# Attention scores of one head at a time, in two halves of the array's rows, in place of head pairs on a block-diagonal key matrix

## The chip, the cores and the metric

The kernel runs on one core of one Trainium2 chip. The metric is the device time of one execution in microseconds (us); lower is better. Three runs of the kernel before took 1596.24 to 1597.06 us, median 1596.8 us.

## What is computed

The reference runs attention with pooled keys and values, then two feed-forward blocks. Cut to what matters here:

```python
B, H, S, D = 8, 8, 576, 64             # pool = 8, so Sp = 72 keys for each head
k_p = k.reshape(B, H, Sp, pool, D).mean(axis=3)
v_p = v.reshape(B, H, Sp, pool, D).mean(axis=3)
scores = scale * np.matmul(q, k_p.transpose(0, 1, 3, 2))
attn = softmax(scores)
x = np.matmul(attn, v_p)               # to 4608 tokens x 512
h = ((x @ w1) * (x @ w2)) @ w3
x2 = h @ w_out
g = softplus(x2 @ w_in)
out = g @ moe2_w_out
```

## The kernel before

**Stages.** The 4608 tokens are 36 attention groups of 128 tokens and 9 blocks of 512 tokens. First (`W_mm`, line 374) the product of w3 and w_out is formed, in plain fp32, while weights arrive by DMA and are converted by ScalarE and VectorE. Then comes the first feed-forward block (`ab`, `x2_mm`, through `mm3`, lines 82 to 84), in which each product is three fp32r matmuls of 128x128 by 512 columns. Attention is spread over both stages: a table of slots (`sched`, filled by `at`) says in which slot each step of each group is recorded, and `p1_step` calls three slots for every 36 matmuls of the feed-forward block. The last stage (`h_mm`, `o_mm`) has no attention in it. Each engine works in the order in which its instructions were recorded.

**One attention group** has, in this order and some slots apart: `scores` (line 205), `softmax` (218), `normalize`, `p_transpose` (line 244, tile `pTp`), `pv` (line 262) and `x_split` (lines 78 and 79, tiles `xh` and `xl`). Four groups are in the first stage, 32 in the feed-forward stage. A group of 128 tokens can straddle two batches, since a batch has 576 tokens: `segments` then returns two pieces of 64 tokens. This is so for 4 of the 36 groups, called crossing groups below; the other 32 are plain.

**Scores.** Queries arrive transposed as `q` [128 rows, 4, 256 tokens]: the rows of slice m are the 64 dimensions of head 2m and the 64 of head 2m+1. `pool_k` sums the raw keys by eight with one VectorE reduction for each m into `ks`, and two ScalarE copies (line 193) put its upper and lower 64 rows on the diagonal of `kT`, whose other blocks were zeroed once by GpSimd (line 337). One matmul of 128 rows, 128 query columns as weights and 144 moving columns then gives two heads (line 213). Four matmuls make a plain group: m = 0 and 1 into the first PSUM tile of the group, m = 2 and 3 into the second. An fp32 matmul is two instructions on the engine, so a plain group has 8 of them, each with its own weight load, and a crossing group 16 (of 64 weight columns).

**PSUM.** `at_p` holds two banks, which scores, transposes and `pv` take in turn. The second score tile of a group is the bank that `pv` of the group before it used, free when `x_split` has read it.

`pv` is a model for the split of the array: head h has its 64 result rows at 64*(h % 2), so even and odd heads multiply in the left and right 64 columns of the array:

```python
r = 64 * (h % 2)
nc.tensor.matmul(ps[r:r + 64, c:c + n], vb_t[b][:, h, :], pT[:, h, o:o + n], start=True, stop=True)
```

Of the kernel before, what the change touches and what calls it, by code (L numbers as in the profile page):

```python
# [8 lines left out]
F32 = mybir.dt.float32  # L9
F32R = mybir.dt.float32r  # L10
I32 = mybir.dt.int32
AF = mybir.ActivationFunctionType
ALU = mybir.AluOpType
AX = mybir.AxisListType

P = 128
B, H, S, D = 8, 8, 576, 64
POOL = 8
SP = S // POOL
# [10 lines left out]
SCALE = 1.0 / (D**0.5 * POOL)  # L30
# [10 lines left out]
def segments(g):  # L41

    b, r = divmod(g * P, S)
    n = min(P, S - r)
    return [(b, 0, n)] + ([(b + 1, n, P - n)] if n < P else [])
# [3 lines left out]
def pooled_attention_two_ffn(ctx: ExitStack, tc: tile.TileContext, qT_d, kT_d, v_d, w12_d, w3T_d, wo_d, wi_d, wo2_d, out):  # L49
# [3 lines left out]
    nc = tc.nc  # L53
# [16 lines left out]
    def at_tile(name):  # L70
        return at_p.tile([P, 512], F32, tag="at", name=name)
# [93 lines left out]
    ap_ = att_stack.enter_context(tc.tile_pool(name="att", bufs=1))  # L165
    q_t, kT_t, vb_t, kv_raw = {}, {}, {}, {}
# [13 lines left out]
            nc.sync.dma_start(t, v_d[b, :, 2 * POOL * D * c:2 * POOL * D * (c + 1)])  # L180
        kv_raw[b, which, c] = t

    kT_bufs = [ap_.tile([P, 4, 2 * SP], F32, tag=f"kT{i}", name=f"kT{i}") for i in range(2)]

    def pool_k(b, m):

        raw = kv_raw.pop((b, 0, m))
        kT_t[b] = kT_bufs[b % 2]
        sums = ap_.tile([P, SP], F32, tag="ksum", name=f"ks{b}_{m}", bufs=2)
        nc.vector.tensor_reduce(sums, raw.rearrange("p (s o) -> p s o", o=POOL), axis=AX.X, op=ALU.add)  # L190
        for i in range(2):
            r = slice(64 * i, 64 * i + 64)
            nc.scalar.activation(kT_t[b][r, m, SP * i:SP * i + SP], sums[r], AF.Copy)

    def pool_v(b, c):

# [6 lines left out]
    sc_t, pr_t, pT_t, pv_t = {}, {}, {}, {}  # L203

    def scores(g):
        q = q_t[g // 2]
        q0 = P * (g % 2)
        sc_t[g] = [at_tile(f"sc{g}_{half}") for half in range(2)]
        for half in range(2):
            ps = sc_t[g][half]  # L210
            for b, o, n in segments(g):
                for m in (2 * half, 2 * half + 1):
                    nc.tensor.matmul(  # L213
                        ps[o:o + n, 2 * SP * (m % 2):2 * SP * (m % 2) + 2 * SP], q[:, m, q0 + o:q0 + o + n], kT_t[b][:, m, :],
                        start=True, stop=True,
                    )

    def softmax(g):
        pr = ap_.tile([P, H, SP], F32, tag="pr", name=f"pr{g}", bufs=2)
        mx = ap_.tile([P, H], F32, tag="mx", name=f"mx{g}", bufs=2)  # L220
        sm = ap_.tile([P, H], F32, tag="sm", name=f"sm{g}", bufs=2)
        sc = [ps[:, :4 * SP].rearrange("p (h n) -> p h n", n=SP) for ps in sc_t.pop(g)]
        for half in range(2):
            nc.vector.tensor_reduce(mx[:, 4 * half:4 * half + 4], sc[half], axis=AX.X, op=ALU.max)
        nc.vector.tensor_scalar(mx, mx, -SCALE, None, op0=ALU.mult)  # L225
        for h in range(H):
            nc.scalar.activation(pr[:, h, :], sc[h // 4][:, h % 4, :], AF.Exp, bias=mx[:, h:h + 1], scale=SCALE, accum_out=sm[:, h:h + 1])  # L227
        pr_t[g] = pr, sm

    def normalize(g):  # L230
# [48 lines left out]
    def kv_step():  # L279
        b, w, c = kv_pieces[kv_pooled[0]]  # L280
        (pool_v if w else pool_k)(b, c)
        kv_pooled[0] += 1
        kv_load_to(kv_pooled[0] + 3)
# [16 lines left out]
    for g in range(NG):  # L300
        o = STEPS_FIRST if g < 4 else STEPS_DENSE if g < 8 or g >= NG - 4 else STEPS
        if o[3] < o[4]:
            at(begin[g] + o[4], lambda g=g: x_split(g))
        at(begin[g], lambda g=g: scores(g))
        at(begin[g] + o[0], lambda g=g: softmax(g))
        at(begin[g] + o[1], lambda g=g: normalize(g))
        at(begin[g] + o[2], lambda g=g: p_transpose(g))
        at(begin[g] + o[3], lambda g=g: pv(g))
        if o[3] == o[4]:
            at(begin[g] + o[3], lambda g=g: x_split(g))  # L310
        if g % 2 == 1 and g // 2 + 3 < NG // 2:
            at(begin[g] + 1, lambda g=g: load_q(g // 2 + 3))
# [20 lines left out]
    with tc.manual_schedule():  # L333
        nc.scalar.preload_act_table_set("natural_log_exp_and_others")
        make_identity(nc, ident)
        for t in kT_bufs:
            nc.gpsimd.memset(t, 0.0)

# [246 lines left out]
        for n in range(len(seq) + LAG):  # L587
            if n < len(seq):
                j, f = seq[n]
# [64 lines left out]
```

## Time and profile before

| | before |
|---|---|
| median of 3 runs | 1596.8 us |
| profiled execution | 1598.61 us |
| its span, first to last instruction | 1596.8 us |
| PE busy (matmul) | 1556.2 us, 97% of the span |
| PEld busy (weight load) | 1254.9 us, 79% |
| VectorE (DVE) / ScalarE (ACT) busy | 853.7 us / 799.7 us |
| mean granted TensorE clock | 0.996 |

Times in the profile are from the first instruction of the span. Matmuls are pipelined: the duration of one matmul instruction reaches past the start of the next, so costs on PE are read from the distance between starts. `L213` is line 213 of the kernel; `sc<-kT,q` is a matmul that writes tile `sc` from tiles `kT` and `q`; `128*64` after a matmul is rows by columns of the array in use, `128x144` what moves through it, and `x8` how many instructions a row merges.

### The profile page before, as it was taken

What the parts mean: (1) busy time and instruction counts of PE and PEld (TensorE: products, weight loads), DVE (VectorE), ACT (ScalarE), POOL (GpSimd) and SP (SyncE); (2) the same over time, 40 slices, a digit from 0 to 9 for tenths busy, and PEclk for the clock granted to TensorE, in tenths of its full rate; (3) what the DMA queues carried; (4) which work ended last, traced back from release to release, by engine and by line L of the source; (5) the groups of instructions that cost most, each with busy time, mean ns of one, the idle gap of its engine ahead of it and who ended that gap; (6) DMA issues with size and microseconds to landing.
All of it is one profiled execution on the core that took longest, in us unless ns stands there. A gap on an engine that the chain in (4) does not pass through costs nothing.

```text
span 1596.8 us, 19269 instructions
## 1 busy us (share of the span) xinstructions
PE 1556.2 (97%) x7424; PEld 1254.9 (79%) x7424; DVE 853.7 (53%) x1452; ACT 799.7 (50%) x1813; POOL 1.7 (0%) x8
## 2 busy tenths in 40 slices
PE   4898999999999999999999999999999999999999
PEld 2457888888888888878878888888888888888887
DVE  6896534243433434327878755555555555555554
ACT  3555433343434343334467665556565565565554
POOL 0000000000000000000000000000000000000000
PEclk9999999999999999999999999999999999999999
DMA  8652212021212111204341101000000001010000
GB/s 275 212 185 76 90 46 66 25 76 37 77 36 63 52 62 29 79 1 158 132 132 54 53 1 53 1 27 27 27 27 27 27 1 53 1 53 1 7 20 27
DMA packets 32011, 95.61 MB, mean 60 GB/s; under 512 B 3632, under 2 KB 3632, under 8 KB 30768
## 3 DMA queue, kind: packets, MB, share of 16 engines
q1 hardware_dynamic: 31920, 94.39, 18.1%
q8 instruction: 58, 0.95, 0.3%
q14 instruction: 33, 0.27, 0.1%
HBM read 75.50 MB, written 18.87 MB: 59 GB/s over the span
## 4 chain that ended last, share of the span: by engine, by line
PE 84%; DVE 8%; ACT 4%; DMA 2%; issue 1%; SPq 0%; ACTq 0%; DVEq 0%
PE ab L82 8%; PE o L573 7%; PE ab L84 7%; PE ab L83 7%; PE o L575 7%; PE o L574 7%; PE h L82 7%; PE h L83 7%; PE h L84 7%; PE x2p L82 4%; PE x2p L84 4%; PE x2p L83 4%; PE sc L213 2%; PE pv L262 2%; PE pTp L244 2%; DMA raw_w<-in_w3T_dram 1%
## 5 line engine op out<-in xcount | busy, mean ns | idle before, releaser
L79 DVE TENSOR_TENSOR g2l<-d,g2h 128x512 fp32r<-128x512 f32 x144 | 99.6, 692 | 328.9 <-ACT g2h L78 328.9
L573 PE MATMUL o<-w2h,g2h 128*128 128x512 f32 x576 | 224.8, 390 | 1.8 <-DVE x2s L445 1.7
L575 PE MATMUL o<-w2h,g2l 128*128 128x512 f32 x576 | 224.2, 389 | 0.0
L574 PE MATMUL o<-w2l,g2h 128*128 128x512 f32 x576 | 224.2, 389 | 0.0
L543 ACT ACTIVATE e<-h 128x512 f32<-128x512 f32 x144 | 85.8, 596 | 270.2 <-PE h L84 270.2
L78 ACT ACTIVATE gh<-g 128x512 fp32r<-128x512 f32 x72 | 45.5, 633 | 179.1 <-DVE g L428 179.1
L573 PEld LDWEIGHTS o<-w2h,g2h 128*128 128x128 f32 x576 | 108.1, 188 | 26.6 <-DVE x2s L445 2.1
L575 PEld LDWEIGHTS o<-w2h,g2l 128*128 128x128 f32 x576 | 108.1, 188 | 23.0 <-DVE g2l L79 0.4
L574 PEld LDWEIGHTS o<-w2l,g2h 128*128 128x128 f32 x576 | 108.1, 188 | 21.8
L82 PE MATMUL x2p<-gh,Wh 128*128 128x512 f32 x288 | 116.1, 403 | 0.0
L84 PE MATMUL x2p<-gh,Wl 128*128 128x512 f32 x288 | 112.6, 391 | 0.0
L83 PE MATMUL x2p<-gl,Wh 128*128 128x512 f32 x288 | 112.3, 390 | 0.0
L227 ACT ACTIVATE pr<-sc,mx 128x72 f32<-128x72 f32 x288 | 87.7, 331 | 48.8 <-DVE mx L225 48.7
L428 DVE TENSOR_TENSOR g<-a,ab 128x512 f32<-128x512 f32 x72 | 49.4, 686 | 108.1 <-PE ab L84 107.0
L553 DVE TENSOR_TENSOR d<-d,l 128x512 f32<-128x512 f32 x144 | 99.7, 692 | 5.0
L552 DVE SCALAR_TENSOR_TENSOR d<-h,d 128x512 f32<-128x512 f32 x144 | 99.6, 692 | 5.0
L551 DVE SCALAR_TENSOR_TENSOR d<-u,e 128x512 f32<-128x512 f32 x144 | 98.7, 685 | 1.0 <-ACT u L546 1.0
L79 DVE TENSOR_TENSOR xl<-pv,xh 128x512 fp32r<-128x512 f32 x36 | 24.8, 690 | 135.5 <-ACT xh L78 135.5
L546 ACT ACTIVATE u<-e 128x512 f32<-128x512 f32 x144 | 91.0, 632 | 10.1 <-DVE d L551 5.7
L548 ACT ACTIVATE l<-u 128x512 f32<-128x512 f32 x144 | 91.1, 633 | 4.7
L544 ACT ACTIVATE e<-e 128x512 f32<-128x512 f32 x144 | 91.0, 632 | 4.6
L78 ACT ACTIVATE g2h<-d 128x512 fp32r<-128x512 f32 x144 | 88.6, 615 | 3.5 <-DVE d L553 2.8
(207 smaller groups left out, 3209.7 us busy)
## 6 DMA issues: line engine op xcount, KB each, us to landing
raw_wo<-in_wo_dram SPq DMA_DIRECT2D x24, 512.0 KB
kv<-in_kT_dram SPq DMA_DIRECT2D x32, 288.0 KB
q<-in_qT_dram SPq DMA_DIRECT2D x18, 512.0 KB
kv<-in_v_dram SPq DMA_DIRECT2D x32, 288.0 KB
x2d<-x2s SPq DMA_DIRECT2D x36, 256.0 KB
x2r<-x2d SPq DMA_DIRECT2D x9, 1024.0 KB
out_dram<-os SPq DMA_DIRECT2D x36, 256.0 KB
raw_w<-in_w3T_dram SPq DMA_DIRECT2D x16, 512.0 KB
```

The lines of the kernel that those rows point to most:

```text
L78: nc.scalar.activation(hi, src, AF.Copy)
L79: nc.vector.tensor_sub(lo, src, hi.bitcast(F32))
L82: nc.tensor.matmul(ps, whi, xhi, start=first, stop=False)
L83: nc.tensor.matmul(ps, whi, xlo, start=False, stop=False)
L84: nc.tensor.matmul(ps, wlo, xhi, start=False, stop=last)
L548: nc.scalar.activation(ln, u, AF.Ln)
L551: nc.vector.scalar_tensor_tensor(d, u, 1.0, e, op0=ALU.subtract, op1=ALU.subtract)
L552: nc.vector.scalar_tensor_tensor(d, ps, 0.0, d, op0=ALU.max, op1=ALU.subtract)
L553: nc.vector.tensor_add(d, d, ln)
L573: nc.tensor.matmul(oacc[j][t], hi[:, s_], wh, start=f == 0, stop=False)
L574: nc.tensor.matmul(oacc[j][t], hi[:, s_], wl, start=False, stop=False)
L575: nc.tensor.matmul(oacc[j][t], lo[:, s_], wh, start=False, stop=f == K2 - 1)
```

## The change

`pool_k` reduces straight into a `kT` tile [128, 4, 72] without zero blocks; the two ScalarE copies, the tile `ks` and the GpSimd zeroing go. `scores` runs over segments, then m, then i: the 64 rows of head 2m+i of the queries against the 64 rows of its keys, 72 moving columns, into PSUM tile i. Even heads are in the first tile of a group and odd heads in the second, and `softmax` reads them from there.

```diff
-    kT_bufs = [ap_.tile([P, 4, 2 * SP], F32, tag=f"kT{i}", name=f"kT{i}") for i in range(2)]
...
-        kT_t[b] = kT_bufs[b % 2]
-        sums = ap_.tile([P, SP], F32, tag="ksum", name=f"ks{b}_{m}", bufs=2)
-        nc.vector.tensor_reduce(sums, raw.rearrange("p (s o) -> p s o", o=POOL), axis=AX.X, op=ALU.add)
-        for i in range(2):
-            r = slice(64 * i, 64 * i + 64)
-            nc.scalar.activation(kT_t[b][r, m, SP * i:SP * i + SP], sums[r], AF.Copy)
+        if m == 0:
+            kT_t[b] = ap_.tile([P, 4, SP], F32, tag="kT", name=f"kT{b}", bufs=2)
+        nc.vector.tensor_reduce(kT_t[b][:, m, :], raw.rearrange("p (s o) -> p s o", o=POOL), axis=AX.X, op=ALU.add)
...
-        sc_t[g] = [at_tile(f"sc{g}_{half}") for half in range(2)]
-        for half in range(2):
-            ps = sc_t[g][half]
-            for b, o, n in segments(g):
-                for m in (2 * half, 2 * half + 1):
+        sc_t[g] = [at_tile(f"sc{g}_{i}") for i in range(2)]
+        for b, o, n in segments(g):
+            for m in range(4):
+                for i in range(2):
+                    r = slice(64 * i, 64 * i + 64)
                     nc.tensor.matmul(
-                        ps[o:o + n, 2 * SP * (m % 2):2 * SP * (m % 2) + 2 * SP], q[:, m, q0 + o:q0 + o + n], kT_t[b][:, m, :],
+                        sc_t[g][i][o:o + n, SP * m:SP * m + SP], q[r, m, q0 + o:q0 + o + n], kT_t[b][r, m, :],
                         start=True, stop=True,
                     )
...
-            nc.scalar.activation(pr[:, h, :], sc[h // 4][:, h % 4, :], AF.Exp, bias=mx[:, h:h + 1], scale=SCALE, accum_out=sm[:, h:h + 1])
+            nc.scalar.activation(pr[:, h, :], sc[h % 2][:, h // 2, :], AF.Exp, bias=mx[:, 4 * (h % 2) + h // 2:4 * (h % 2) + h // 2 + 1], scale=SCALE, accum_out=sm[:, h:h + 1])
...
-        for t in kT_bufs:
-            nc.gpsimd.memset(t, 0.0)
```

On TensorE, a plain group in the feed-forward stage. Before, two matmuls for each PSUM tile stand between `ab` and `x2p` (names end in buffer numbers, a row's size is what the matmul writes):

```order
L84 MATMUL ab_2_1_941<-xh_276,w_3l 128x512
L213 MATMUL sc_0_960<-kT_83,q_198 128x144 x2
L213 MATMUL sc_1_961<-kT_83,q_198 128x144 x2
L82 MATMUL x2p_0_860<-gh_1_847,Wh_708 128x512
```

With the change:

```order
L84 MATMUL ab_2_1_939<-xh_265,w_3l 128x512
L211 MATMUL sc_0_958<-kT_440,q_183 128x72
L211 MATMUL sc_1_959<-kT_440,q_183 128x72
L211 MATMUL sc_0_958<-kT_440,q_183 128x72
L211 MATMUL sc_1_959<-kT_440,q_183 128x72
L211 MATMUL sc_0_958<-kT_440,q_183 128x72
L211 MATMUL sc_1_959<-kT_440,q_183 128x72
L211 MATMUL sc_0_958<-kT_440,q_183 128x72
L211 MATMUL sc_1_959<-kT_440,q_183 128x72
L82 MATMUL x2p_0_858<-gh_1_845,Wh_698 128x512
```

The place between its neighbours is the same; four matmuls became eight, and the two PSUM tiles alternate from the first one on.

On TensorE, the first crossing group. Before, the two batches (`kT_82` and `kT_83`) alternate by two matmuls:

```order
L213 MATMUL sc_0_777<-kT_82,q_198 64x144 x2
L213 MATMUL sc_0_777<-kT_83,q_198 64x144 x2
L213 MATMUL sc_1_778<-kT_82,q_198 64x144 x2
L213 MATMUL sc_1_778<-kT_83,q_198 64x144 x2
```

With the change all eight of one batch come ahead of the eight of the other; here from the seventh to the tenth of the sixteen:

```order
L211 MATMUL sc_0_767<-kT_123,q_183 64x72
L211 MATMUL sc_1_768<-kT_123,q_183 64x72
L211 MATMUL sc_0_767<-kT_440,q_183 64x72
L211 MATMUL sc_1_768<-kT_440,q_183 64x72
```

On ScalarE, the start of the program. Before, six copies to `kT` stand ahead of the first conversion of w3:

```order
L100 ACTIVATE wgh_512_115<-raw_wo_1_101 128x512
L193 ACTIVATE kT_82<-ks_0_127 64x72 x2
L193 ACTIVATE kT_82<-ks_1_133 64x72 x2
L193 ACTIVATE kT_82<-ks_2_139 64x72 x2
L100 ACTIVATE wgh_512_149<-raw_w_0_0_103 128x512
```

With the change they are gone, and the conversion follows the one before it:

```order
L100 ACTIVATE wgh_512_111<-raw_wo_1_97 128x512
L100 ACTIVATE wgh_512_137<-raw_w_0_0_99 128x512
```

## Rows read from the trace of the kernel before

**Rows 1.** The page's first part: busy us (share of the span) and instructions by engine.
```profile
PE 1556.2 (97%) x7424; PEld 1254.9 (79%) x7424; DVE 853.7 (53%) x1452; ACT 799.7 (50%) x1813; POOL 1.7 (0%) x8
```

**Rows 2.** Table of stretches: length, PE, PEld, DVE, ACT, POOL busy; clock, DMA share, GB/s.
```profile
0.00:40.00 40.00, 18.76 (x46) 9.44 (x48) 27.28 (x52) 13.28 (x37) 1.73 (x8) 0.92 0.84 275
...
300.00:400.00 100.00, 100.00 (x533) 82.31 (x532) 36.47 (x66) 36.41 (x126) 0.00 (x0) 1.00 0.15 45
```

**Rows 3.** What PE waited for: us in total, times, longest.
```profile
PE Wp L374 <- DVE wgh L111: 16.9, 1, 16.9
PE pTp L244 <- DVE pr L235: 11.9, 6, 4.3
PE sc L213 <- DVE xl L79: 5.1, 3, 2.2
```

**Rows 4.** PE's timeline around a plain scores block: start us, us, instruction, count.
```profile
299.66 0.39 PE L83 MATMUL ab<-xl,w_3h 128*128 128x512 f32 x1
...
301.95 0.39 PE L84 MATMUL ab<-xh,w_3l 128*128 128x512 f32 x1
302.18 1.14 PE L213 MATMUL sc<-kT,q 128*128 128x144 f32 x8
...
303.40 0.40 PE L83 MATMUL x2p<-gl,Wh 128*128 128x512 f32 x1
```

**Rows 5.** PE's timeline, two stretches of matmuls of the first stage.
```profile
98.25 1.88 PE L374 MATMUL Wp<-wgh,wgh 128*128 128x512 f32 x4
99.96 1.88 PE L374 MATMUL Wp<-wgh,wgl 128*128 128x512 f32 x4
```

**Rows 6.** PE's timeline around the pv block of a plain group.
```profile
317.51 0.39 PE L84 MATMUL ab<-xh,w_4l 128*128 128x512 f32 x1
317.83 1.09 PE L262 MATMUL pv<-pT,vb 72*64 72x128 f32 x16
...
319.19 0.40 PE L83 MATMUL ab<-xl,w_5h 128*128 128x512 f32 x1
```

**Rows 7.** PE's timeline around the pv block of a crossing group.
```profile
127.17 0.39 PE L84 MATMUL ab<-xh,w_2l 128*128 128x512 f32 x1
127.48 1.15 PE L262 MATMUL pv<-pT,vb 72*64 72x64 f32 x32
...
128.90 0.39 PE L83 MATMUL ab<-xl,w_3h 128*128 128x512 f32 x1
```

**Rows 8.** PE's timeline around the scores block of a crossing group.
```profile
110.96 0.39 PE L84 MATMUL ab<-xh,w_1l 128*128 128x512 f32 x1
111.28 1.25 PE L213 MATMUL sc<-kT,q 128*64 128x144 f32 x16
...
112.80 0.40 PE L83 MATMUL ab<-xl,w_0h 128*128 128x512 f32 x1
```

**Rows 9.** PEld's timeline: the first two weight loads after a pv block.
```profile
318.85 0.19 PEld L82 LDWEIGHTS ab<-xh,w_5h 128*128 128x128 f32 x1 [0.17 <-issue]
318.96 0.19 PEld L83 LDWEIGHTS ab<-xl,w_5h 128*128 128x128 f32 x1
```

**Rows 10.** Groups by line and shape: count | busy us, mean ns | idle before, releaser.
```profile
L213 PEld LDWEIGHTS sc<-kT,q 128*128 128x128 f32 x256 | 37.2, 196 | 10.0 <-DVE xl L79 5.7 <-issue 2.2
L262 PEld LDWEIGHTS pv<-pT,vb 72*64 72x64 f32 x640 | 31.6, 138 | 15.2 <-issue 11.7 <-ACT pT L245 2.3 <-ACT wgh L100 0.8
L193 ACT ACTIVATE kT<-ks 64x72 f32<-64x72 f32 x64 | 16.7, 261 | 39.6 <-DVE ks L190 39.2
```

**Rows 11.** PE's timeline: a scores block of the first stage that waits.
```profile
40.75 0.76 PE L213 MATMUL sc<-kT,q 128*128 128x144 f32 x4
43.73 1.33 PE L213 MATMUL sc<-kT,q 128*128 128x144 f32 x4 [2.22 <-DVE xl L79]
```

**Rows 12.** DVE's timeline near the start.
```profile
13.42 0.98 DVE L103 TENSOR_SCALAR wgh<-wgh 128x512 f32<-128x512 f32 x2 [1.28 <-ACT wgh L100]
```

**Rows 13.** The chain that ended last, near the start: start us, us, what.
```profile
12.73 0.24 ACT wgh L100
12.97 9.53 DMA raw_w<-in_w3T_dram
```

## The prediction

> **What bounds the kernel now.** I read the busy shares first [rows 1]: PE is busy 97% of the span, no other engine much over half. The table of stretches [rows 2] says where that fails: in the first 40 us PE has 18.76 us of work and DMA a share of 0.84, while at 300 to 400 us PE is busy all 100 us at a granted clock of 1.00, its 2.4 GHz level, with DVE and ACT near 36 us each. PE's waits [rows 3] agree: 33.9 us in these three lines, of which all but some 5 us lie before 124 us. So there are two regimes. Up to about 124 us a chain of DMA, ACT, DVE and PE sets the pace; after it whatever lengthens or shortens PE's own stream moves the end by as much. 28 of the 32 plain score blocks stand in the second regime, and of the 4 crossing ones all but the first, which at 111 us comes shortly before; 4 plain ones stand in the first.
>
> Busy times on PE overlap, so I price a block by starts: from the last fp32r matmul ahead of it to the second one behind it, less two ordinary steps. An ordinary step is (301.95 - 299.66) / 10 = 0.229 us [rows 4].
>
> - Plain scores: 303.40 - 301.95 - 0.458 = **0.992 us** [rows 4].
> - Crossing scores: 112.80 - 110.96 - 0.458 = **1.382 us** [rows 8].
> - `pv`, plain: 319.19 - 317.51 - 0.458 = **1.222 us** [rows 6]; `pv`, crossing: 128.90 - 127.17 - 0.458 = **1.272 us** [rows 7].
>
> **What an instruction costs.** Four fp32 instructions of 512 columns take 99.96 - 98.25 = 1.71 us [rows 5], so one streams at 0.428 / 512 = 0.835 ns a column: 0.120 us for 144 columns, 0.107 for 128, 0.060 for 72. Plain scores are then 8 x 0.120 = 0.962 us of streaming and 0.030 us of anything else: the array never pauses, and every weight load is hidden. The zero blocks cost half of that streaming, and this is what the change goes for.
>
> A weight load of 128 columns takes 318.96 - 318.85 = 0.11 us where two follow each other with no matmul in the way [rows 9]. One of 64 columns takes about half: the loads' latencies differ by 196 - 138 = 58 ns [rows 10], and in the crossing `pv` 16 pairs of instructions with 64 moving columns (0.053 us of streaming) take (1.272 - 0.367) / 16 = 0.057 us a pair [rows 7], with the 0.367 of the next paragraph. These loads have 72 or 128 rows [rows 7, 8] and cost the same: columns set the price, not rows. The same pairs show that the two halves of a split array load and multiply side by side.
>
> **What a split costs.** Plain `pv` is 8 pairs of 0.107 us = 0.855 us; the other 1.222 - 0.855 = 0.367 us is what it pays to go into a split array and back (the first load and the emptying of the array lie bare). The crossing scores pay 1.382 - 8 x 0.120 = 0.420 us. Plain scores, unsplit, pay 0.030.
>
> **The change on PE, plain group.** 4 matmuls become 8, 8 instructions with a load become 16, in two row halves of 8 each. In one half a step is the longer of streaming 0.060 us and the load of 128 query columns, 0.11 us: **the load, which was hidden under 0.120 us of streaming, becomes the bound**. With the halves side by side: 8 x 0.11 = 0.88 us, the last matmul 0.060, and the price of the split without its first short load, 0.367 - 0.053 = 0.314. Sum 1.254 us, against 0.992: +0.262 us, and for 28 blocks **+7.3 us**.
>
> Bounds. No row shows a split by rows. Its price lies between nothing (0.030, as unsplit) and 0.420; I take `pv`'s, the nearest row. Then a block is 0.91 to 1.31 us. If row halves load faster than any row here, streaming would bound: 0.053 + 8 x 0.060 + 0.314 = 0.85 us with the price, 0.51 without. If the loads of the halves come one after another: 16 x 0.11 + 0.060 + 0.314 = 2.13 us.
>
> The Trainium skill (TensorEngine Tiling (Array Packing), Key Properties) says that a change of the tiling mode, and not merely of the tile, drains TensorE. By it a split by rows pays as a split by columns does, and the sum is the +7.3 us above; the rows here show it for columns only. The same page (Overview, Theoretical Speedup) promises up to 2x for a small dimension of 64; by that a block would take the 0.85 or 0.51 us above, which no row on weight loads supports.
>
> **Crossing group.** It is split already, and goes from two column halves to four quarters. Eight steps bound by streaming (0.060 us, the load is 0.055): with all four side by side 0.055 + 0.48 + 0.314 = 0.85 us, with one batch after the other 1.33 us; 4 blocks give -2.1 or -0.2 us. Before, the two batches ran side by side (16 instructions in 8 steps [rows 8]) though they stood in turns of two matmuls; now eight stand ahead. I take the middle, **-1.2 us**.
>
> **The first stage.** Three of its four score blocks wait for `xl` to free the second bank [rows 3, 11]. Before, half of the block ran ahead of that wait; now the second matmul needs that bank, so 14 of 16 instructions run behind it. Behind the wait stood 4 x 0.120 us = 0.48; now 7 x 0.11 + 0.060 and part of the split's price, about +0.4 us each, which also delays the Wp matmuls queued behind and the maxima on DVE. ScalarE sheds 64 copies, 16.7 us [rows 10], none of which PE waits for later; but six stand ahead of the first w3 conversion, and DVE idles 1.28 us for it [rows 12]. What follows is a DMA of 9.53 us that the chain hangs on that same ACT step [rows 13], which takes some of this back. I take **+0.7 us**, within -1.3 and +2. In the second regime no score block waits for a bank (the three waits are the first stage's), and the removed GpSimd zeroing and shorter ACT work are hidden under PE. DVE's reductions keep their number and size; they now wait for the matmuls that read `kT` two batches earlier, long done.
>
> **Sum.** 7.3 - 1.2 + 0.7 = **+6.8 us**. The profiled execution took 1598.61 us (span 1596.8) and would take 1605.4; the median of the runs shown is 1.8 us lower, so I forecast **1603.6 us**. With a price of the split between 0.24 and 0.42 us, and the first stage at its worst for the latter, this case spans about 1600 to 1608.
>
> **Rivals.**
> - **A split by rows costs nothing (ends faster).** Nothing shows it, nothing excludes it: the array keeps its 128 columns, unlike in `pv`. Block 0.91 us: 28 x -0.082 = -2.3, crossing -1.2, first stage 0: 1593.3 us. It decides as soon as the price falls under some 0.05 us; at half the price and a little less the result is no measurable change. Chance 0.15, and 0.08 for a price in between that leaves it within 0.2%.
> - **Loads no longer bind.** 28 x (0.85 - 0.992) - 2.1 = -6 us with the price of the split, 1591; -15 us without, 1582. Against it: loads of 72 and of 128 rows cost alike. Chance 0.08.
> - **The halves load one after another.** 28 x 1.14 = +32, crossing (32 loads of 0.055) +3, first stage +4: 1636 us. Against it: column halves load together [rows 7]. Chance 0.08.
> - **A load waits for the matmul of its own half.** 8 x (0.11 + 0.060) + 0.314 = 1.67 us a block, in all +20: 1617 us. Against it: in every block above loads hide under matmuls on the same rows. Chance 0.06. The Trainium skill (TensorE: Matmul & The Clock Gate, Part 3, The mechanism) says in its list of what overlaps that a load overlaps matmuls in flight only where the row group differs, though the text ahead of the list also names a background weight buffer; read strictly the list is this rival, and the unsplit blocks of this trace speak against that reading.
>
> **How the numbers follow.** The forecast has 0.55, of which 0.04 within 0.2% (3.2 us, about what a measurement of this kernel can tell from no change). Slower: 0.51 + 0.08 + 0.06 = 0.65. Same: 0.04 + 0.08 + 0.03 (of the first rival) = 0.15. Faster: 0.12 + 0.08 = 0.20. The range takes the forecast, the first rival and the cases between: 1592 to 1610; outside are the two expensive rivals and most of the second.
>
> **What would show it.** In the new profile a plain block priced as above should be near 1.25 us, with starts of one half 0.11 us apart, starts of the two halves a few ns apart, and a bare gap ahead of its first load, as `pv` has; crossing blocks 0.85 to 1.33 us; everything after about 720 us unchanged in length; no new wait of `sc` for `xl` past 124 us. A block under 0.95 us, or one over 1.6 us, makes the forecast wrong.

## The result, and the profile after

The changed kernel takes 1608.68 us (median of 4 runs, 1607.76 to 1610.69) against 1596.93 us (4 runs). The ratio is 1.0069, 95% interval 1.0048 to 1.0090: slower by 7.7 to 14.4 us, where +6.8 us was forecast. The median lies in the range of the forecast (1592 to 1610) and 5 us above its 1603.6. Five more runs beside another set of the kernel before gave 1.0059 (1.0047 to 1.0071). The profiled execution, 1607.76 us, is the fastest of the four; its span is 1606.0 us, 9.2 us over that of before.

Page of the changed kernel, first part, which answers to [rows 1]:

```profile
PE 1565.4 (97%) x7744; PEld 1253.7 (78%) x7744; DVE 853.8 (53%) x1452; ACT 783.8 (49%) x1749; POOL 0.7 (0%) x6
```

PE has 320 matmul instructions more, ScalarE 64 instructions and 16 us less, and PE is busy 9 us longer. `e1` and `e2` below show no gain from what left ScalarE; the blocks show what came to PE.

PE's timeline around the plain scores block that answers to [rows 4] (start us, us, instruction, count), and the weight loads of the same block:

```profile
307.20 0.39 PE L84 MATMUL ab<-xh,w_3l 128*128 128x512 f32 x1
307.52 1.11 PE L211 MATMUL sc<-kT,q 64*128 64x72 f32 x16
308.57 0.50 PE L82 MATMUL x2p<-gh,Wh 128*128 128x512 f32 x1
308.90 0.39 PE L83 MATMUL x2p<-gl,Wh 128*128 128x512 f32 x1
```

```profile
307.52 0.97 PEld L211 LDWEIGHTS sc<-kT,q 64*128 64x128 f32 x16 [0.35 <-issue]
308.56 0.19 PEld L82 LDWEIGHTS x2p<-gh,Wh 128*128 128x128 f32 x1
308.67 0.19 PEld L83 LDWEIGHTS x2p<-gl,Wh 128*128 128x128 f32 x1
```

By the measure of the prediction (less two steps of 0.227 us, as they run around 307 us) the block costs 308.90 - 307.20 - 0.454 = 1.25 us; all 28 plain blocks of the feed-forward stage give 1.248 us within 1 ns. Forecast: 1.254. The first load stands behind 0.35 us in which nothing is loaded, as `pv`'s does. Single starts in the trace: the two halves of a pair 7 ns apart, pairs 0.112 us apart.

The first crossing block, against [rows 8]:

```profile
113.04 0.39 PE L84 MATMUL ab<-xh,w_1l 128*128 128x512 f32 x1
113.35 1.03 PE L211 MATMUL sc<-kT,q 64*64 64x72 f32 x32
114.31 0.50 PE L82 MATMUL ab<-xh,w_0h 128*128 128x512 f32 x1
114.66 0.40 PE L83 MATMUL ab<-xl,w_0h 128*128 128x512 f32 x1
```

114.66 - 113.04 - 0.454 = 1.17 us, against 1.39 before by the same measure: between the two bounds (0.85 and 1.33), nearer the upper.

PE's waits, against [rows 3], and PE's timeline in the first stage: the Wp matmuls that wait for `wgl`, and the second scores block, against [rows 11]:

```profile
PE Wp L370 <- DVE wgh L111: 15.3, 1, 15.3
PE pTp L242 <- DVE pr L233: 10.9, 6, 3.1
PE sc L211 <- DVE xl L79: 6.8, 3, 3.8
```

```profile
26.29 5.40 PE L370 MATMUL Wp<-wgh,wgl 128*128 128x512 f32 x8 [1.95 <-DVE wgl L111]
39.76 0.44 PE L211 MATMUL sc<-kT,q 64*128 64x72 f32 x2
43.96 1.78 PE L211 MATMUL sc<-kT,q 64*128 64x72 f32 x14 [3.76 <-DVE xl L79]
```

Two instructions of the block and no longer four run ahead of its wait, and PE idles 3.76 us in place of 2.22. Stretches of the changed kernel behind it (the number after the five engines is the granted clock as a share of 2.4 GHz):

```profile
44.00:48.00 4.00, 4.00 (x17) 2.71 (x18) 3.34 (x7) 1.46 (x10) 0.00 (x0) 0.53 0.49 146
48.00:52.00 4.00, 4.00 (x7) 1.58 (x6) 2.83 (x8) 2.17 (x10) 0.00 (x0) 0.62 0.94 358
124.00:132.00 8.00, 6.15 (x48) 4.97 (x50) 5.38 (x12) 1.78 (x3) 0.00 (x0) 0.79 0.23 68
```

The kernel before has 0.64, 1.00 and 1.00 in these three stretches. Its lines for the first stretch and for the Wp matmuls in it, and the same matmuls of the changed kernel:

```profile
44.00:48.00 4.00, 4.00 (x9) 2.25 (x10) 2.97 (x7) 2.09 (x15) 0.00 (x0) 0.64 0.73 243
44.85 6.34 PE L374 MATMUL Wp<-wgl,wgh 128*128 128x512 f32 x12
```

```profile
45.67 8.07 PE L370 MATMUL Wp<-wgl,wgh 128*128 128x512 f32 x12
```

**Where the 9.2 us lie.** Four places of PE's timeline, before and after: the first `ab` matmul, the transposes of the first crossing group, the first plain block of the second regime, and the plain block behind that of [rows 4]:

```profile
105.60 0.50 PE L82 MATMUL ab<-xh,w_0h 128*128 128x512 f32 x1 [0.32 <-DVE Wl L79]
123.75 1.04 PE L244 MATMUL pTp<-ident,pr 128*72 128x128 f32 x8 [2.80 <-DVE pr L235]
131.42 1.14 PE L213 MATMUL sc<-kT,q 128*128 128x144 f32 x8
321.71 1.14 PE L213 MATMUL sc<-kT,q 128*128 128x144 f32 x8
```

```profile
107.69 0.50 PE L82 MATMUL ab<-xh,w_0h 128*128 128x512 f32 x1
125.85 1.63 PE L242 MATMUL pTp<-ident,pr 128*72 128x128 f32 x8 [3.04 <-DVE pr L233]
135.20 1.11 PE L211 MATMUL sc<-kT,q 64*128 64x72 f32 x16
327.27 1.11 PE L211 MATMUL sc<-kT,q 64*128 64x72 f32 x16
```

- Up to the first `ab` matmul, the first stage: +2.1 us.
- From there to the transposes: nothing. The crossing block between them is 0.22 us shorter, but the transposes wait for `pr`, and the wait grows from 2.80 to 3.04 us.
- From there to the first plain block: +1.7 us more, +3.8 in all. TensorE's granted clock is 0.79 from 124 to 132 us, and 1.00 in the kernel before. This is not the split's: `e1`, whose matmuls are those of the kernel before, has such a spell too (0.88), and PE falls back by 1.3 us in it. The second trace of the changed kernel has none: there the lag is +3.7 us at the first `ab` matmul (109.33 us) and +3.8 at the first plain block.
- From there to the end: 9.2 - 3.8 = +5.4 us. A plain group's period went from 321.71 - 302.18 = 19.53 us to 327.27 - 307.52 = 19.75: +0.22 us, while the block alone grew by 0.255. The matmuls behind an unsplit block run a few ns slower each, some ten of them, against five or six behind a split one, which gives some 0.03 us back.

### The profile page after: what moved, and what is told of

Its sections match the earlier page's. It is cut to its first block, busy times and chain, and to the rows that moved or that the text cites. A ratio compares the mean times of both kernels' runs of the same rounds, so it can differ in the third digit from the quotient of the medians.

```text
span 1606.0 us, 19806 instructions
## 1 busy us (share of the span) xinstructions
PE 1565.4 (97%) x7744; PEld 1253.7 (78%) x7744; DVE 853.8 (53%) x1452; ACT 783.8 (49%) x1749; POOL 0.7 (0%) x6
## 4 chain that ended last, share of the span: by engine, by line
PE 87%; DVE 5%; ACT 3%; DMA 2%; issue 1%; SPq 0%; ACTq 0%; DVEq 0%
PE o L569 8%; PE o L571 8%; PE o L570 8%; PE h L84 8%; PE h L83 8%; PE h L82 8%; PE ab L82 8%; PE ab L83 7%; PE ab L84 7%; PE x2p L82 4%; PE x2p L84 3%; PE x2p L83 3%; PE sc L211 2%; PE pv L260 2%; PE pTp L242 2%; ACT pr L225 1%
## 5 line engine op out<-in xcount | busy, mean ns | idle before, releaser
L421 ACT ACTIVATE a<-ab 128x512 f32<-128x512 f32 x72 | 43.0, 598 | 102.2 <-PE ab L84 72.2
```

## The experiments

Block costs below are by the measure of the prediction, with steps of 0.227 us.

**What sets the step of 0.112 us.** `e4` makes each head's keys 120 columns wide:

```diff
+NW = 120
...
+    kT_bufs = [ap_.tile([P, 4, NW], F32, tag=f"kT{i}", name=f"kT{i}") for i in range(2)]
...
-                        sc_t[g][i][o:o + n, SP * m:SP * m + SP], q[r, m, q0 + o:q0 + o + n], kT_t[b][r, m, :],
+                        sc_t[g][i][o:o + n, NW * m:NW * m + NW], q[r, m, q0 + o:q0 + o + n], kT_t[b][r, m, :],
...
+        for t in kT_bufs:
+            nc.gpsimd.memset(t, 0.0)
```

`pool_k` then fills the first 72 columns of each head, and `softmax` reads only these.

> The changed kernel, but 120 moving columns for each head (72 keys and 48 zero columns that are not used) in place of 72. If the load of 128 query columns sets the step of a row half (theory), the step stays at 0.112 us, since 120 columns stream in 0.100 us, and a plain block grows only by its last matmul: 1.248 + 48 x 0.835 ns = 1.29 us. Rival: the step of 0.112 us is streaming that is slower in a split array (1.55 ns a column); then 120 columns take 0.187 us and a block 8 x 0.187 + 0.31 = 1.81 us. Crossing blocks, whose loads take half, grow in both: from 1.17 to about 1.5 us.

Plain block of `e4`, PE's timeline:

```profile
306.89 0.39 PE L85 MATMUL ab<-xh,w_3l 128*128 128x512 f32 x1
307.20 1.16 PE L213 MATMUL sc<-kT,q 64*128 64x120 f32 x16
308.29 0.50 PE L83 MATMUL x2p<-gh,Wh 128*128 128x512 f32 x1
308.63 0.39 PE L84 MATMUL x2p<-gl,Wh 128*128 128x512 f32 x1
```

308.63 - 306.89 - 0.454 = 1.29 us. Two thirds more columns cost 0.04 us, that of the last matmul. The rival's 1.81 is out: streaming is hidden in a step. That a step is the load of 128 weight columns, and not a fixed time of an instruction, shows in the crossing block of `e6`, where 64 columns are loaded: the steps of one quarter are 0.0625 us apart. And with loads of 64 columns the moving columns do count: the crossing blocks of `e4` cost 1.65 us, against 1.17 in the changed kernel, where about 1.5 was expected. The one run of `e4` took 1609.10 us.

**Loads without the split.** `e5` is the kernel before with every matmul cut in two:

```diff
-                    nc.tensor.matmul(
-                        ps[o:o + n, 2 * SP * (m % 2):2 * SP * (m % 2) + 2 * SP], q[:, m, q0 + o:q0 + o + n], kT_t[b][:, m, :],
+                    for i in range(2):
+                        c = 2 * SP * (m % 2) + SP * i
+                        nc.tensor.matmul(
+                            ps[o:o + n, c:c + SP], q[:, m, q0 + o:q0 + o + n], kT_t[b][:, m, SP * i:SP * i + SP],
...
```

> The kernel before, with each matmul of 144 moving columns cut into two of 72 and nothing else: 16 instructions on all 128 rows, no split. Theory (loads bind, and it is the two halves loading side by side that keeps the changed kernel from worse): 16 loads of 0.11 us in a row, 16 x 0.11 + 0.06 = 1.8 us a plain block against 0.992, in all some +23 us, about 1620 us; no bare gap ahead of the block. Rival (the split's price alone makes the change slow, loads are hidden): 16 x 0.060 + 0.03 = 0.99 us and no change.

```profile
312.22 0.39 PE L84 MATMUL ab<-xh,w_3l 128*128 128x512 f32 x1
312.45 1.90 PE L215 MATMUL sc<-kT,q 128*128 128x72 f32 x16
314.15 0.48 PE L82 MATMUL x2p<-gh,Wh 128*128 128x512 f32 x1
314.46 0.39 PE L83 MATMUL x2p<-gl,Wh 128*128 128x512 f32 x1
```

```profile
312.22 1.98 PEld L215 LDWEIGHTS sc<-kT,q 128*128 128x128 f32 x16
```

314.46 - 312.22 - 0.454 = 1.79 us, without a gap ahead of the first load, and 1626.42 us in all against 1601.24 us of the kernel before in one run beside it: +25 us, where some +23 was expected. Sixteen loads in a row cost 1.79, 0.112 each; eight pairs, side by side, 8 x 0.112 = 0.90 of the changed kernel's 1.25. The halves do load together, and the load is what binds in both. It takes 0.112 us on 128 rows here and on 64 in the changed kernel. In the kernel before, where starts are 0.122 us apart, the 144 columns of two heads hid it.

**The price of the split.** `e7` issues every score matmul of the changed kernel twice:

```diff
-            for m in range(4):
+            for m in (0, 1, 2, 3, 0, 1, 2, 3):
```

> The changed kernel with every score matmul issued twice (the second overwrites the first with the same numbers). Theory: the price of the split is paid once a block, steps are 0.112 us: 1.248 + 8 x 0.112 = 2.14 us a plain block, and the price is 1.248 - 8 x 0.112 - 0.06 = 0.29 us. Rival: part of the 0.29 us is paid for each change between the halves; then 2.14 to 2.5 us.

```profile
320.55 0.39 PE L84 MATMUL ab<-xh,w_3l 128*128 128x512 f32 x1
320.87 2.01 PE L211 MATMUL sc<-kT,q 64*128 64x72 f32 x32
322.80 0.50 PE L82 MATMUL x2p<-gh,Wh 128*128 128x512 f32 x1
323.14 0.39 PE L83 MATMUL x2p<-gl,Wh 128*128 128x512 f32 x1
```

323.14 - 320.55 - 0.454 = 2.14 us, as expected. Eight more steps cost 0.89 us, 0.112 each (2.141 - 1.248, means of the 28 blocks), and 1.248 - 0.894 - 0.060 = 0.29 us is paid once for each block, the same at both lengths. The total, one run, was 1641.24 us.

**Crossing groups.** `e6` has the batches in turn:

```diff
-        for b, o, n in segments(g):
-            for m in range(4):
+        for m in range(4):
+            for b, o, n in segments(g):
```

> The changed kernel with the batches of a crossing group innermost but one (for m, for segment, for i), so that the four quarters of the array get matmuls in turn. Theory (1.167 us because the second batch is recorded 16 instructions behind and starts late): 0.055 + 8 x 0.0625 + 0.31 = 0.87 us a crossing block, plain blocks unchanged, in all 4 x 0.3 = -1.2 us against the changed kernel. Rival (four quarters can't run at once): 1.17 us or more.

```profile
113.41 0.39 PE L84 MATMUL ab<-xh,w_1l 128*128 128x512 f32 x1
113.73 0.73 PE L211 MATMUL sc<-kT,q 64*64 64x72 f32 x32
114.39 0.50 PE L82 MATMUL ab<-xh,w_0h 128*128 128x512 f32 x1
114.73 0.40 PE L83 MATMUL ab<-xl,w_0h 128*128 128x512 f32 x1
```

114.73 - 113.41 - 0.454 = 0.87 us in place of 1.17: four quarters work side by side once their instructions stand near each other. In the second crossing block of the changed kernel the second batch, 16 instructions behind, starts 0.31 us after the first (288.07 and 287.76 us), which is about the difference. The single run, 1607.54 us, can't show the 1.2 us.

**The two parts of the change, and the first stage.** These four were run on one chip beside 17 runs of the kernel before (median 1598.63 us, 1595.32 to 1601.81).

> The changed kernel once more, beside the next three on the same chip, for the runs and the traces of its first 135 us. Theory: the steady part gives 28 x 0.256 - 4 x 0.22 = +6.3 us in every run; what is above that is the first stage, which may differ from run to run.

Measured: 1607.77 us, ratio 1.0059 (1.0047 to 1.0071). Blocks as before, 1.248 and 1.167 us; the first plain block of the second regime at 135.25 us.

`e1`, ScalarE relieved (GpSimd makes the copies), matmuls as before:

```diff
-            nc.scalar.activation(kT_t[b][r, m, SP * i:SP * i + SP], sums[r], AF.Copy)
+            nc.gpsimd.tensor_copy(kT_t[b][r, m, SP * i:SP * i + SP], sums[r])
```

> The kernel before with the 64 copies to the diagonal of kT on GpSimd in place of ScalarE: the change's relief of ScalarE alone, score matmuls as before. Theory: ScalarE's 16.7 us are hidden but for the six copies ahead of the first w3 conversion; the first Wp matmul starts some 1.5 us earlier (15.3 in place of 16.9 us), DMA takes it back, and the end moves by -1 to 0 us. Rival: the relief is worth several us through the first stage, -2 us or more.

Measured: ratio 1.0010 (0.9998 to 1.0022). Wp starts 1.1 us earlier, at 15.83 us; in its trace 0.5 us of that is left at the first `ab` matmul, and in the total none that the runs can tell. The rival's -2 us is out.

`e2`, the split alone: `pool_k` and `kT` are those of the kernel before, `scores` and `softmax` those of the change but for the keys' place (here against the line of the changed kernel):

```diff
-                        sc_t[g][i][o:o + n, SP * m:SP * m + SP], q[r, m, q0 + o:q0 + o + n], kT_t[b][r, m, :],
+                        sc_t[g][i][o:o + n, SP * m:SP * m + SP], q[r, m, q0 + o:q0 + o + n], kT_t[b][r, m, SP * i:SP * i + SP],
```

> The changed kernel's matmuls on the old block-diagonal kT, filled by the old ScalarE copies: the split alone. Theory: plain block 1.248 us and crossing 1.167 as in the changed kernel; first stage at best 1 us worse than it. In all +9 to +13 us against the kernel before. Rival (the relief matters): 2 us or more over the changed kernel.

Measured: ratio 1.0063 (1.0051 to 1.0076), about +10 us, not to be told from the changed kernel. The split carries the change, as far as the runs can tell.

`e8`, the first four groups as before, with their block-diagonal keys and ScalarE copies:

```diff
...
+        if g < 4:
+            for half in range(2):
+                ps = sc_t[g][half]
+                for m in (2 * half, 2 * half + 1):
+                    nc.tensor.matmul(
+                        ps[:, 2 * SP * (m % 2):2 * SP * (m % 2) + 2 * SP], q[:, m, q0:q0 + P], kT0[:, m, :],
+                        start=True, stop=True,
+                    )
+            return
...
```

> The changed kernel with the four groups of the first stage (batch 0) done as before: block-diagonal keys, ScalarE copies, no split. Theory (all over +6.3 us comes from the first stage's split blocks, whose work stands behind the wait for the second bank): +6.3 us against the kernel before, about 1603 us, and the sc blocks of the first stage at their old times. Rival (the rest comes from elsewhere, the clock or the stretch from 110 to 135 us): as slow as the changed kernel, +9 to +12 us.

Measured: 1604.15 us, ratio 1.0032 (1.0020 to 1.0044), +5.1 us (3.2 to 7.0), where +6.3 was expected. The first plain block of the second regime is back at 132.08 us. The four split blocks of the first stage thus cost the other 4 us (9.4 - 5.1), some 1 us each, four times the 0.26 of a block in steady work. The two intervals leave 0.4 to 1.8 us a block (an estimate). `e8` also brings the ScalarE copies of the first batch back, which by `e1` and `e2` makes no difference that the runs can tell.

The traces at hand agree, by the start of the first `ab` matmul, which stands ahead of the spell at 1.2 GHz. It is at 104.59 to 106.20 us in the kernel before, `e1`, `e8` and `e9`, without a split in the first stage, and at 107.53 to 110.24 us in both traces of the changed kernel, `e2`, `e3`, `e4` and `e6`, with it.

**Why so much there.** `e3` changes the order within these four groups alone:

```diff
+        order = [(m, i) for i in range(2) for m in range(4)] if g < 4 else [(m, i) for m in range(4) for i in range(2)]
...
+            for m, i in order:
...
```

> The changed kernel, where the four groups of the first stage do their four even heads first and their four odd heads behind them, so that 8 instructions and not 2 are recorded ahead of the wait for the second bank. Theory (PE idles longer at that wait, 3.8 us in place of 2.2 in the second group, and the granted clock is at its 1.2 GHz level for longer behind it): the idle time falls by about 0.8 us, the clock in 48 to 52 us is near 1.00 again, and PE's lag at the second transpose block falls from about +3 to about +1.5 us, the whole by 1 to 2 us to about 1606. Rival (it is the work recorded behind the wait): 8 odd heads' steps of 0.112 us are as long as the 7 pairs of steps were, and nothing changes.

PE's timeline and a stretch of `e3`:

```profile
40.86 1.11 PE L211 MATMUL sc<-kT,q 64*128 64x72 f32 x8
44.69 1.11 PE L211 MATMUL sc<-kT,q 64*128 64x72 f32 x8 [2.72 <-DVE xl L79]
```

```profile
48.00:52.00 4.00, 4.00 (x9) 1.71 (x8) 2.50 (x8) 2.52 (x12) 0.00 (x0) 0.84 0.83 258
```

The wait fell to 2.72 us, the clock in that stretch rose from 0.62 to 0.84, and the second transpose block came 0.9 us earlier than in the changed kernel. The total did not follow: 1.0057 (1.0044 to 1.0070). What was won in the second group was lost again by the transposes of the third (69.41 us, against 68.62 in the changed kernel), at a granted clock of 0.79 from 62 to 70 us, where the changed kernel has 1.00. Nor is the lag a matter of the clock alone: over the first 105 us `e3` has 0.95, the kernel before 0.93, and its first `ab` matmul still comes 1.9 us later.

`e11` frees the bank earlier, by one slot:

```diff
-    STEPS_FIRST = (1, 2, 4, 5, 6)
+    STEPS_FIRST = (1, 2, 4, 5, 5)
```

> The changed kernel with x_split of the first four groups recorded in the slot of pv, one slot earlier on ScalarE and VectorE, so that the second bank is free earlier. Theory (what the first stage costs beyond the steady part, some 3 us, hangs on the wait of the split blocks for that bank): PE's waits of sc for xl fall from 6 to 7 us to under 4, PE's lag at the first ab matmul falls from between +1.9 and +3.7 us (against the trace of the kernel before) to about +1, and the whole is 1 to 2 us faster than the changed kernel. Rival (it hangs on the blocks being longer, wherever the bank comes free): the lag stays at +2 or more.

PE's timeline and two stretches of `e11`:

```profile
39.73 0.44 PE L211 MATMUL sc<-kT,q 64*128 64x72 f32 x2
42.15 1.11 PE L211 MATMUL sc<-kT,q 64*128 64x72 f32 x14 [1.97 <-DVE xl L79]
```

```profile
44.00:48.00 4.00, 4.00 (x10) 1.71 (x9) 2.73 (x7) 2.34 (x16) 0.00 (x0) 1.00 0.70 271
48.00:52.00 4.00, 4.00 (x17) 2.24 (x16) 3.71 (x10) 2.51 (x7) 0.00 (x0) 1.00 0.65 222
```

The waits for the bank fell to 2.7 us in all, the clock stayed at 2.4 GHz in these two stretches, and the first `ab` matmul came 3.0 us ahead of the kernel before, where the two traces of the changed kernel are 2.1 and 3.7 us behind. That execution took 1601.08 us; the other five of the same kernel took 1605.80 to 1607.96 us, and the ratio, 1.0046 (1.0029 to 1.0063), overlaps that of the changed kernel. So this trace is that of an unusually fast execution. It points at the wait for the bank as the place of the loss, but the runs don't show that an earlier bank recovers it.

**A version that might beat both.** `e9` is the kernel before with its crossing groups alone in quarters, batches in turn:

```diff
+        if len(segments(g)) == 2:
+            for m in range(4):
+                for b, o, n in segments(g):
+                    for i in range(2):
+                        r = slice(64 * i, 64 * i + 64)
+                        nc.tensor.matmul(
+                            sc_t[g][i][o:o + n, SP * m:SP * m + SP], q[r, m, q0 + o:q0 + o + n], kT_t[b][r, m, SP * i:SP * i + SP],
+                            start=True, stop=True,
+                        )
+            return
...
```

> The kernel before, with its four crossing groups alone done in quarters of the array, batches in turn, and plain groups on all 128 rows as before: a version that should beat both kernels. Theory: a crossing block is split already and pays for it either way, so 1.386 falls to 0.87 us; the rest is unchanged; 4 x -0.5 = -2 us, at the edge of what the runs can tell from no change. Rival (quarters among unsplit groups cost something elsewhere): no change or slower.

Its first crossing block, PE's timeline:

```profile
111.55 0.39 PE L84 MATMUL ab<-xh,w_1l 128*128 128x512 f32 x1
111.87 0.73 PE L214 MATMUL sc<-kT,q 64*64 64x72 f32 x32
112.53 0.50 PE L82 MATMUL ab<-xh,w_0h 128*128 128x512 f32 x1
112.87 0.40 PE L83 MATMUL ab<-xl,w_0h 128*128 128x512 f32 x1
```

The crossing blocks cost 112.87 - 111.55 - 0.454 = 0.87 us in place of 1.39, and each of the last three brings PE 0.52 us forward against the kernel before. The first brings nothing: PE's lag is +0.6 us at the first `ab` matmul, +0.1 behind the block, and +0.6 again at the transposes that wait for `pr`. The total, 0.9997 (0.9986 to 1.0008) over 11 runs, can't be told from it. `e12` adds the step of `e11`:

> The same step on the version with quartered crossing groups and everything else as before. Theory: the unsplit blocks wait 5 to 7 us in the first stage too and gain by it; with the -2 us of the crossing groups 2 to 4 us faster than the kernel before. Rival: DMA and the conversions on VectorE set the pace of the first stage, x_split earlier delays them, and the total is as before.

Measured: 1597.21 us over 12 runs beside 1599.79 us, ratio 0.9989 (0.9976 to 1.0002). It is the fastest version tried, by 1.8 us in the middle of the interval, and the interval still holds no change. In its trace the first `ab` matmul is at 103.64 us, 2.0 us ahead of the kernel before, so an earlier bank goes with an earlier end of the first stage without the split as well.

## Why the prediction was right, and where it was off

- **Plain block, +0.262 us:** right in size (1.248 for 1.254 us) and in each part. The load as the bound (0.112 us a step) is shown by `e4` and `e5`, the halves loading side by side by `e5`, a price of the split paid once a block by `e7` (0.29 for 0.314 us). That columns and not rows set the price of a load, [rows 7, 8] could not show, since in rows 8 the load is hidden; `e5` does (0.112 us on 128 rows as on 64). The Trainium skill says that a change of the tiling mode drains TensorE (TensorEngine Tiling (Array Packing), Key Properties). The traces agree for a split by rows, which no row of before could show: nothing is loaded for 0.35 us ahead of the block, and `e7` gives the whole a price of 0.29 us here.
- **28 blocks, +7.3 us:** 28 x 0.22 = 6.1 us by the period of a group. The price was read from starts too close behind the block; the matmuls further on give some 0.03 us back.
- **Crossing groups, -1.2 us:** 4 x (1.167 - 1.386) = -0.9 us by the blocks, and about -0.7 by PE's starts, since the first of them is followed by a wait and brings nothing. That the block would fall between the two bounds was a guess; the reason named for it holds: the second batch starts late, and side by side (`e6`) the lower bound of 0.85 us is reached (0.87).
- **First stage, +0.7 us, from -1.3 to +2: the term that was mis-sized, beyond its own range.** The changed kernel's traces are 2.1 and 3.7 us late at the first `ab` matmul, and `e8` puts about 4 us of the total on the four split blocks there. "About +0.4 us each" counted the work behind the wait for the second bank and nothing that follows from it. What the trace shows beside it: PE idles 3.76 us in place of 2.22 ahead of that work, since only 2 instructions precede the wait, and the 12 Wp instructions behind the block take 8.07 us in place of 6.34, at a lower granted clock. How much of the 4 us these two carry is not shown. The start of Wp came 1.7 us earlier, as argued (DVE no longer idles 1.28 us), but the next Wp matmuls, which wait 1.95 us for `wgl`, start at 26.29 us, against 26.18 before. The second transpose block comes 2.5 us late (55.29 us, against 52.75).
- **ScalarE's relief, nearly all hidden:** right, as far as the runs can tell (`e1`, `e2`).
- **Other signs:** as said. `sc` waits for `xl` three times, all in the first stage, and PE's lag is the same at 720 us and at the end.
- **Rivals:** all fell. The split by rows has its price (`e7`), loads bind (`e4`), halves load together (`e5`), and a load doesn't wait for the matmul of its own half, since steps are 0.112 and not 0.17 us.

In sum, for the profiled execution: +2.1 us in the first stage, +1.7 with the spell at 1.2 GHz, which no row of before shows, then 6.1 - 3 x 0.22 = +5.4, together +9.2 us, the difference of the two spans. In the second trace it is 3.7, 0.1 and 5.4. The median of the first four runs lies 2.6 us further off, and is just above the 1600 to 1608 us that the prediction gave to its own case. The direction and the main term are shown. That the sum is no further off is in part luck: the plain blocks were put 1.2 us too high, the first stage 1.4 to 3 us too low. Open is how the first stage turns four longer blocks into 4 us: `e5`, unsplit and with blocks longer by 0.8 us, is late by 3.6 us at the first `ab` matmul as well, so it need not be the split itself; `e3` and `e11` move the wait and the clock in their traces without a clear change of the total.

## What to carry to other kernels

Zeros that stream while the next weights load are nearly free: before halving what moves through the array, compare a step's streaming with the load of its weights, which here went by their columns (0.112 us for 128) and not by their rows. Here the split brought a step from 0.122 to 0.112 us only, and cost 0.29 us a block: an estimate from these is that some 30 steps in a row would have to pay for it, and a block has 8. Such a price weighs nothing where, as in the crossing groups, it is paid already. In a stage where engines wait for each other in a ring, a block can cost several times its own growth (some 1 us for 0.26 here), and a block ahead of a wait for another engine can gain nothing by being shorter, so such stretches are priced apart.

## What the runs showed of the hardware that was not expected

- TensorE's granted clock differs between executions of like kernels, and the length of an idle time alone does not tell it. Around 44 to 48 us it was 0.64 after an idle time of 2.22 us (before), 0.53 after 3.76 us (changed kernel), 1.00 after 1.97 us (`e11`). At the transposes of the first crossing group PE idles 3.04 us in both traces of the changed kernel: from 124 to 132 us the one has 0.79, the other 1.00.
- That spell at 1.2 GHz (0.82 to 0.94 of full speed from 124 to 140 us) is in the first trace of the changed kernel, `e1`, `e6`, `e7`, `e8`, `e9` and `e12`, and in none of the kernel before, the second trace of the changed kernel, `e2`, `e3`, `e4`, `e5` or `e11`: it comes with and without the split. `e9`'s PE lost 2.6 us there against the kernel before. Runs of the kernel before alone spread over 1595 to 1603 us.
- How far matmuls of different parts of the array overlap hangs on how near their instructions are in the program: 2 matmuls apart they started together (the crossing block before: starts 13 ns apart), 8 apart 0.31 us late.
- The first ten or so full-array matmuls behind a block without a split run slower by a few ns each (steps up to 0.236 in place of 0.227 us); behind a split one it is five or six.
